# Gated linear attention and a three-way maxout FFN: units of 64 tokens of two batches in 64x64 array tiles, 32x32 blocks turned by VectorE, all engine orders fixed

## The chip, the cores and the metric

The kernel runs on one core of a Trainium2 chip. The metric is device time in microseconds (us), as the median of several executions. A core has five engines with an instruction stream each: TensorE (PE in the profile; PEld is its weight load), VectorE (DVE), ScalarE (ACT), GpSimd (POOL) and SyncE (SP), which here does little but issue DMA transfers. SyncE's issues stand in the traces shown here in the order of its program.

## The reference

Attention with a gated state, per batch and head, followed by an FFN whose hidden layer is the largest of three products. All inputs are float32 or float64 arrays as below; the weights arrive in float64 and are rounded on the chip.

```python
# B, H, S, D = 4, 8, 768, 48;  d_model = H*D = 384;  d_ff = 768
f = 1.0 / (1.0 + np.exp(-f_logit))
for t in range(S):
    state = f[:, :, t, :, None] * state + np.einsum('bhd,bhe->bhde', k[:, :, t], v[:, :, t])
    y[:, :, t] = np.einsum('bhd,bhde->bhe', q[:, :, t], state)
x = np.ascontiguousarray(y.transpose(0, 2, 1, 3)).reshape(B * S, H * D)      # 3072 x 384
h = np.maximum(np.maximum(x @ w1, x @ w2), x @ w3)
out = h @ w_out
```

## The kernel before

The sequence is cut into chunks of C = 128 tokens. One unit is one chunk of one batch; there are 24 units, and four units (the four batches at the same chunk) make one group of 512 tokens for the FFN. Per unit: f, k and q are loaded with tokens on partitions and turned by TensorE (`gates`), a scan gives the running products of the gates, a reciprocal gives the scaled keys `kh`; then come scores (`pairs`), values, the state and its read (`outputs`). The result is moved into `xT`, the FFN's input, by ten DMA transfers per unit. The FFN is a generator: each `next` (called by `fill`) emits one step, so that a group's FFN is mixed among the attention units of the next group.

```python
def load(u):
    c, b = divmod(u, B)
    for nm, src in (("f", f_logit), ("k", k), ("q", q), ("v", v)):
        nc.sync.dma_start(out=pads[nm][u % NLD][:, :, 0:D], in_=src[b, :, c*C:(c+1)*C, :].rearrange("h t d -> t h d"))
# ... in outputs(u, xT):
    for hp in range(HP):
        for par in range(2):
            nc.tensor.matmul(y[par*DP:(par+1)*DP, hp, :], lhsT=v_ld[:, 2*hp+par, :], rhs=at[:, par, hp, :], ...)
# ... key state, state read, then:
    nc.scalar.copy(yT, y)
    for h in range(H):               # ten transfers per unit, over borders of 128 rows
        # ...
        nc.sync.dma_start(out=xT[row % 128:row % 128 + n, row // 128, b*C:(b+1)*C], in_=yT[p0:p0+n, h // 2, :])
# ... the main loop, orders left to the scheduler:
for u in range(NU):
    # ...
    fill(2); pairs(u); fill(1); outputs(u, xT)
    if u + NLD < NU: load(u + NLD)
    # ... gates of later units, three weight pieces rounded in the first group
    fill(2)
    if u % GRP == GRP - 1:
        for _ in pending: pass
        pending = ffn(u // GRP, xT)
```

Of the kernel before, what the change touches and what calls it, by code (L numbers as in the profile page):

```python
# [34 lines left out]
C = 128  # L35
DP = 64
# [7 lines left out]
def kernel(  # L44
# [15 lines left out]
    NCH = S // C  # L60
    NU = B * NCH
# [4 lines left out]
    GRP = B  # L66
    TOK = GRP * C

    const = ctx.enter_context(tc.tile_pool(name="const", bufs=1))
    ident = const.tile([128, 128], FP32, name="ident")  # L70
    make_identity(nc, ident)
    w_in = [const.tile([128, NK, DFF], FP32, name=f"w_in{i}") for i in range(3)]
# [3 lines left out]
    def fast():  # L76
        ctx = ExitStack()
        with ctx:
# [7 lines left out]
            mask = keep.tile([C, C], FP32, name="mask")  # L86
            nc.gpsimd.memset(mask, 1.0)
            nc.gpsimd.affine_select(out=mask, in_=mask, compare_op=ALU.is_ge, fill=0.0, base=0,
                                    pattern=[[1, C]], channel_multiplier=-1)


            floor = keep.tile([128, HP, C + 1], FP32, name="floor")
            nc.vector.memset(floor, P_FLOOR)
            nc.vector.memset(floor[:, :, 0], 1.0)
            gate_tiles = [keep.tile([128, HP, C + 1], FP32, name=f"gate{i}") for i in range(2)]
# [4 lines left out]
            ends = keep.tile([128, NU, HP], FP32, name="ends")  # L100

            NLD = 4
            pads = {}
            for nm, pad in (("f", GATE_PAD), ("k", 0.0), ("q", 0.0), ("v", 0.0)):
                pads[nm] = []
                for i in range(NLD):
                    t = keep.tile([C, H, DP], FP32, name=f"{nm}_ld{i}")
                    nc.vector.memset(t[:, :, D:DP], pad)
                    pads[nm].append(t)


            def load(u):
                c, b = divmod(u, B)
                for nm, src in (("f", f_logit), ("k", k), ("q", q), ("v", v)):
                    nc.sync.dma_start(out=pads[nm][u % NLD][:, :, 0:D],
                                      in_=src[b, :, c * C:(c + 1) * C, :].rearrange("h t d -> t h d"))


            pieces = [(w_in[i][:, :, j * 128:(j + 1) * 128],
                       src[:, j * 128:(j + 1) * 128].rearrange("(kt p) c -> p kt c", p=128))  # L120
                      for j in range(NJ) for i, src in enumerate((moe_w1, moe_w2, moe_w3))]
            pieces += [(w_out[:, j:j + 1, :], moe_w_out[j * 128:(j + 1) * 128, :].rearrange("(j p) c -> p j c", p=128))
                       for j in range(NJ)]
            N = DM
            RAW = 6
            raw = {}

            def load_weight(n):
                if n >= len(pieces):
                    return  # L130
                dst, src = pieces[n]
                if src.dtype == FP32:
                    nc.sync.dma_start(out=dst, in_=src)
                else:
                    raw[n] = work.tile([128, 2 * N], U32, name="raw", bufs=RAW)
                    nc.sync.dma_start(out=raw[n].rearrange("p (a c) -> p a c", a=dst.shape[1]),
                                      in_=src.bitcast(U32))

            def round_weight(n):
                if n in raw:  # L140
                    dst = pieces[n][0]
                    words = raw.pop(n).rearrange("p (n two) -> p n two", two=2)
                    lo, hi = words[:, :, 0], words[:, :, 1]


                    top = work.tile([128, N], U32, name="top_bits")
                    nc.vector.tensor_scalar(top, hi, 3, 0x3FFFFFF8, op0=ALU.logical_shift_left, op1=ALU.bitwise_and)  # L147
                    nc.vector.scalar_tensor_tensor(top, hi, 0xC0000000, top, op0=ALU.bitwise_and, op1=ALU.bitwise_or)  # L148

                    rest = work.tile([128, N], U32, name="rest_bits")  # L150
                    nc.scalar.activation(rest, lo, AF.Copy, scale=2.0 ** -29)
                    nc.vector.tensor_tensor(top, top, rest, op=ALU.add)  # L152


                    size = work.tile([128, N], FP32, name="size")
                    nc.scalar.activation(size, hi.bitcast(FP32), AF.Square)
                    a = dst.shape[1]
                    nc.vector.scalar_tensor_tensor(dst, size.rearrange("p (a c) -> p a c", a=a), HI_MIN ** 2,
                                                   top.bitcast(FP32).rearrange("p (a c) -> p a c", a=a),
                                                   op0=ALU.is_ge, op1=ALU.mult)  # L160
                load_weight(n + RAW)


            def transposed(x):
                t = ps_tr.tile([128, HP, C], FP32, name="tr")
# [3 lines left out]
                return t  # L169

            ready = {}

            def gates(u):
                f_ld, k_ld, q_ld = (pads[nm][u % NLD] for nm in "fkq")
                tr_f = transposed(f_ld)
                gate = gate_tiles[u % 2]
                nc.scalar.activation(gate[:, :, 1:], tr_f, AF.Sigmoid)  # L177
                scan = work.tile([128, HP, C + 1], FP32, name="prod", bufs=3)
                nc.vector.tensor_tensor_scan(scan.rearrange("p a t -> p (a t)"), gate.rearrange("p a t -> p (a t)"),  # L179
                                             floor.rearrange("p a t -> p (a t)"), 1.0, op0=ALU.mult, op1=ALU.max)  # L180
                prod = scan[:, :, 1:]
                inv = work.tile([128, HP, C], FP32, name="inv")
                nc.vector.reciprocal(inv, prod)  # L183
                tr_k = transposed(k_ld)
                kt = work.tile([128, HP, C], FP32, name="kt")
                nc.scalar.copy(kt, tr_k)
                tr_q = transposed(q_ld)
                qt = work.tile([128, HP, C], FP32, name="qt")
                nc.scalar.copy(qt, tr_q)  # L189
                kh = work.tile([128, HP, C], FP32, name="kh", bufs=3)  # L190
                nc.gpsimd.tensor_tensor(kh, kt, inv, op=ALU.mult)  # L191
                qh = work.tile([128, HP, C], FP32, name="qh", bufs=3)
                nc.gpsimd.tensor_tensor(qh, qt, prod, op=ALU.mult)  # L193
                nc.gpsimd.tensor_copy(ends[:, u, :], prod[:, :, C - 1])  # L194
                ready[u] = (prod, kh, qh)

            def pairs(u):
                c = u // B
                prod, kh, qh = ready[u]
                a = ps_a.tile([C, 2, HP, C], FP32, name="a")  # L200
                for hp in range(HP):
                    for par in range(2):
                        r = slice(par * DP, par * DP + D)
                        nc.tensor.matmul(a[:, par, hp, :], lhsT=kh[r, hp, :], rhs=qh[r, hp, :],  # L204
                                         start=True, stop=True)
                at = work.tile([C, 2, HP, C], FP32, name="at")
                for par in range(2):
                    nc.vector.tensor_tensor(at[:, par], a[:, par],  # L208
                                            mask.unsqueeze(1).to_broadcast([C, HP, C]), op=ALU.mult)
                ks = None  # L210
                if c < NCH - 1:
                    tr_s = ps_tr.tile([C, HP, 128], FP32, name="tr")
                    for hp in range(HP):
                        nc.tensor.transpose(tr_s[:, hp, :], kh[:, hp, :], ident)  # L214
                    ks = work.tile([C, H, DP], FP32, name="ks")
                    nc.scalar.copy(ks.rearrange("s h d -> s (h d)"), tr_s.rearrange("s a d -> s (a d)"))  # L216
                ready[u] = (prod, qh, at, ks)

            states = [[keep.tile([128, HP, D], FP32, name=f"st{b}_{i}") for i in range(2)] for b in range(B)]

            def outputs(u, xT):
                c, b = divmod(u, B)
                prod, qh, at, ks = ready.pop(u)
                v_ld = pads["v"][u % NLD]
                st, st_new = states[b][c % 2], states[b][(c + 1) % 2]
                y = ps_y.tile([128, HP, C], FP32, name="y")
                for hp in range(HP):
                    for par in range(2):
                        nc.tensor.matmul(y[par * DP:(par + 1) * DP, hp, :], lhsT=v_ld[:, 2 * hp + par, :],  # L229
                                         rhs=at[:, par, hp, :], start=(hp == 0),  # L230
                                         stop=(c == 0 and hp == HP - 1), skip_group_check=True)
                if c < NCH - 1:
                    ds = ps_tr.tile([128, HP, D], FP32, name="tr")
                    for hp in range(HP):
                        for par in range(2):
                            nc.tensor.matmul(ds[par * DP:(par + 1) * DP, hp, :], lhsT=ks[:, 2 * hp + par, :],  # L236
# [322 lines left out]
```

## Time and profile before

| | before |
|---|---|
| median of 4 runs (of the rounds shared with the changed kernel) | 555.74 us (554.5 to 556.89) |
| span of the profiled run, mean granted TensorE clock | 553.3 us, 0.964 |
| first FFN matmul starts | 68.7 us |
| first group of units after that, then four groups | 82.6, then 83.4 each |
| last FFN and tail | 61.9 and 6.7 |

The prediction shows how these come out of the profile.

### The profile page before, as it was taken

Reading aid. Unit: us, or ns where it says so; the run is one execution under the profiler, and the core shown is the slowest. Engines: PE = TensorE matmul, PEld = TensorE weight load, DVE = VectorE, ACT = ScalarE, POOL = GpSimd, SP = SyncE. Lnnn points to the kernel's source line nnn. Section 1 sums busy time; section 2 is a strip of 40 time slices with the busy share of each in tenths; the row PEclk is TensorE's granted clock in tenths of the full one; section 3 lists DMA queues with packets and bytes.
Section 4 is the critical chain, followed back from the end, with each engine's and each line's share of the span. In section 5 each row is a group of like instructions: output and inputs, shape, how many; then the busy total and the mean of one; then the engine's idle time right before and its main releaser. Section 6 shows DMA issues: what was moved, by which queue, how often, KB each, and the median us from issue to landing. Waiting matters only on the chain.

```text
span 553.3 us, 7062 instructions
## 1 busy us (share of the span) xinstructions
PE 525.2 (95%) x2714; PEld 297.6 (54%) x2714; DVE 248.2 (45%) x322; ACT 121.9 (22%) x225; POOL 66.5 (12%) x82
## 2 busy tenths in 40 slices
PE   5886899998999999999999999999999999999995
PEld 4664644545655555555555555655655555544452
DVE  7799935995055435054346054346044242011210
ACT  3353422551122112122212122212122210110010
POOL 4322200220011001011011011011011010000000
PEclk9686889997999999999999999999999999999998
DMA  9857676353232213123122223130200000100001
GB/s 182 228 113 154 157 202 156 103 138 62 78 73 57 62 35 63 58 58 72 41 51 53 64 65 71 28 64 11 58 28 15 12 9 10 57 14 1 0 14 50
DMA packets 124458, 38.31 MB, mean 69 GB/s; under 512 B 104448, under 2 KB 123648, under 8 KB 124416
## 3 DMA queue, kind: packets, MB, share of 16 engines
q1 hardware_dynamic: 124416, 37.77, 28.4%
q8 instruction: 23, 0.38, 0.3%
q14 instruction: 19, 0.16, 0.1%
HBM read 28.31 MB, written 4.72 MB: 60 GB/s over the span
## 4 chain that ended last, share of the span: by engine, by line
PE 85%; DVE 8%; issue 3%; ACT 2%; POOL 1%; DVEq 0%; ACTq 0%; POOLq 0%
PE p L273 47%; PE p L286 17%; PE tr L168 5%; PE a L204 4%; PE y L229 4%; PE y L242 3%; DVE inv L183 3%; PE tr L236 2%; PE tr L214 2%; DVE prod L179 1%; POOL kh L191 1%; DVE at L208 1%; DVE top_bits L148 1%; DVE top_bits L152 1%; DVE top_bits L147 1%
## 5 line engine op out<-in xcount | busy, mean ns | idle before, releaser
L273 PE MATMUL p<-xT,w_in 128*128 128x512 f32 x648 | 292.7, 598 | 0.0
L273 PEld LDWEIGHTS p<-xT,w_in 128*128 128x128 f32 x648 | 118.0, 190 | 126.4 <-issue 123.7
L286 PE MATMUL p<-w_out,hm 128*128 128x384 f32 x288 | 96.3, 495 | 0.0
L183 DVE RECIPROCAL inv<-prod 128x512 f32<-128x512 f32 x24 | 80.4, 3351 | 1.8
L286 PEld LDWEIGHTS p<-w_out,hm 128*128 128x128 f32 x288 | 55.2, 193 | 39.1 <-issue 3.3
L279 DVE TENSOR_TENSOR top<-p,top 128x512 f32<-128x512 f32 x36 | 24.6, 682 | 112.4 <-PE p L273 112.4
L179 DVE TENSOR_TENSOR_SCAN prod<-gate,floor 128x516 f32<-128x516 f32 x24 | 29.5, 1229 | 90.0 <-ACT gate L177 88.0
L277 ACT COPY top<-p 128x512 f32<-128x512 f32 x36 | 21.1, 586 | 129.0 <-PE p L273 128.9
L279 DVE TENSOR_TENSOR hm<-p,top 128x512 f32<-128x512 f32 x36 | 24.6, 683 | 48.6 <-PE p L273 48.3
L194 POOL COPY ends<-prod 128x4 f32<-128x4 f32 x24 | 5.1, 213 | 321.4 <-DVE prod L179 321.4
L204 PEld LDWEIGHTS a<-qh,kh 48*128 48x128 f32 x384 | 25.3, 193 | 25.9 <-issue 16.8
L204 PE MATMUL a<-qh,kh 48*128 48x128 f32 x384 | 31.4, 295 | 8.0 <-POOL kh L191 8.0
L191 POOL TENSOR_TENSOR kh<-kt,inv 128x512 f32<-128x512 f32 x24 | 32.1, 1336 | 37.8 <-DVE inv L183 36.7
L208 DVE TENSOR_TENSOR at<-a,mask 128x512 f32<-128x512 f32 x48 | 31.0, 681 | 9.7 <-PE a L204 9.7
L229 PE MATMUL y<-at,v_ld 128*64 128x128 f32 x384 | 32.4, 301 | 2.5 <-DVE at L208 2.2
L229 PEld LDWEIGHTS y<-at,v_ld 128*64 128x64 f32 x384 | 24.3, 150 | 18.7 <-issue 14.1
L245 ACT COPY yT<-y 128x512 f32<-128x512 f32 x24 | 14.0, 585 | 83.7 <-PE y L242 78.7
L289 ACT COPY o<-p 128x384 f32<-128x384 f32 x24 | 11.5, 479 | 88.8 <-PE p L286 88.8
L193 POOL TENSOR_TENSOR qh<-qt,prod 128x512 f32<-128x512 f32 x24 | 28.3, 1181 | 21.2 <-ACT qt L189 21.2
L242 PE MATMUL y<-qh,st 48*48 48x128 f32 x320 | 23.0, 283 | 0.0
L216 ACT COPY ks<-tr 128x512 f32<-128x512 f32 x20 | 11.7, 586 | 50.1 <-PE tr L214 50.1
L177 ACT ACTIVATE gate<-tr 128x512 f32<-128x512 f32 x24 | 14.3, 597 | 36.5 <-PE tr L168 36.5
(45 smaller groups left out, 282.4 us busy)
## 6 DMA issues: line engine op xcount, KB each, us to landing
raw<-in_moe_w_dram SPq DMA_DIRECT2D x18, 384.0 KB, 4.8
f_ld<-in_f_logit_dram SPq DMA_DIRECT2D x24, 192.0 KB, 2.9
k_ld<-in_k_dram SPq DMA_DIRECT2D x24, 192.0 KB, 3.4
q_ld<-in_q_dram SPq DMA_DIRECT2D x24, 192.0 KB, 3.5
v_ld<-in_v_dram SPq DMA_DIRECT2D x24, 192.0 KB, 3.0
out_dram<-o SPq DMA_DIRECT2D x24, 192.0 KB, 1.9
xT<-yT SPq DMA_DIRECT2D x144, 24.0 KB, 1.8
raw<-in_moe_w_out_dram SPq DMA_DIRECT2D x6, 384.0 KB, 3.6
```

The lines of the kernel that those rows point to most:

```text
L168: nc.tensor.transpose(t[:, hp, :], flat[:, hp * 128:(hp + 1) * 128], ident)
L179: nc.vector.tensor_tensor_scan(scan.rearrange("p a t -> p (a t)"), gate.rearrange("p a t -> p (a t)"), floor.rearrange("p a t -> p (a t)") ...
L183: nc.vector.reciprocal(inv, prod)
L191: nc.gpsimd.tensor_tensor(kh, kt, inv, op=ALU.mult)
L193: nc.gpsimd.tensor_tensor(qh, qt, prod, op=ALU.mult)
L204: nc.tensor.matmul(a[:, par, hp, :], lhsT=kh[r, hp, :], rhs=qh[r, hp, :], start=True, stop=True)
L208: nc.vector.tensor_tensor(at[:, par], a[:, par], mask.unsqueeze(1).to_broadcast([C, HP, C]), op=ALU.mult)
L229: nc.tensor.matmul(y[par * DP:(par + 1) * DP, hp, :], lhsT=v_ld[:, 2 * hp + par, :], rhs=at[:, par, hp, :], start=(hp == 0), stop=(c == 0 ...
L242: nc.tensor.matmul(y[r, hp, :], lhsT=st[r, hp, :], rhs=qh[r, hp, :], start=False, stop=(hp == HP - 1), skip_group_check=True)
L273: nc.tensor.matmul(p, lhsT=w_in[i][:, kt, j * 128:(j + 1) * 128], rhs=xT[:, kt, :], start=(kt == 0), stop=(kt == NK - 1))
L279: nc.vector.tensor_tensor(hm[:, j, :] if i == 2 else top, p, top, op=ALU.max)
L286: nc.tensor.matmul(p[:, 0:DM], lhsT=hm[:, j, i * C:(i + 1) * C], rhs=w_out[:, j, :], start=(j == 0), stop=(j == NJ - 1))
```

## The change

The intent is to make TensorE's attention work cheaper and the start shorter. A unit becomes 64 tokens of two batches, so that each small product has four 64x64 array tiles to run in. From unit 8 on, f, k and q are loaded as blocks of 32x32 so that VectorE can turn them instead of TensorE. Rows of `xT` and the input weights are permuted, so that most of the result reaches `xT` by ScalarE copies and only six small transfers per unit are left. The weights' add moves to GpSimd. And everything stands in one manual schedule: the program's order is each engine's order.

```diff
-C = 128
+C = 64                                 # UT = 2*C token rows of a unit; GRP = 4
 # ...
+            elif u % 2 == 0:           # BY_ROWS = 8: later units by 32x32 blocks, two units at once
+                for n in range(C // 32):
+                    for par in range(2):
+                        for e0, w in ((0, 32), (32, D - 32)):
+                            nc.sync.dma_start(out=blocks[nm][u // 2 % 2][p0:p0 + 32, n, :, 0:w], in_=...)
 # ... in round_weight:
-    nc.vector.tensor_tensor(top, top, rest, op=ALU.add)
+    nc.gpsimd.tensor_tensor(top, top, rest, op=ALU.add)
 # ... in products(u):
-    tr_k = transposed(k_ld); nc.scalar.copy(kt, tr_k)
+    turned(t, block(nm, u))            # nc.vector.transpose, units 8 and later
 # ... every attention product:
-    for hp in range(HP):
-        for par in range(2):
+    FOUR = [(par, a) for a in range(2) for par in range(2)]
+    for hp in range(HP):
+        for par, a in FOUR:
 # ... in finish(u, xT):
-    ten nc.sync.dma_start(out=xT[...], in_=yT[...])
+    for par in range(2):               # after ScalarE copies of the other rows
+        for i in range(NK):
+            nc.sync.dma_start(out=xT[p0 + D:p0 + DP, i, t0:t0 + UT], in_=last[...])
 # ... the order:
+with tc.manual_schedule():
+    # loads of units 0 to 3, four weight pieces; gates(0); gates(1)
+    for u in range(GRP):
+        keys(u)
+        if u > 1: finish(u - 1, xT)
+        pairs(u)
+        if u + 2 < GRP: gates(u + 2)
+        values(u)
+        load(u + GRP); load_v(u + GRP)
+        # finish(0) at u == 0; three weight pieces at u == 1
+    finish(GRP - 1, xT)
+    pending = ffn(0, xT)
+    # ...
+    for u in range(GRP, NU):
+        if BY_ROWS <= u + 2 < NU and u % 2 == 0: load(u + 2)
+        # load_v(u + 2)
+        fill(2 if u % 2 and u < NU - GRP else 1)
+        keys(u)
+        if u > GRP: finish(u - 1, xT)
+        if u % GRP == 0:
+            if u > GRP:
+                fill(99)
+                pending = ffn(u // GRP - 1, xT)
+            xT = new_xT()
+        pairs(u)
+        # ... sigmoids, products, values, quotients of units u and u + 1, with fill(1) between
```

(The lines of the diff are shortened; the cuts are marked by `# ...`.)

## The prediction

> **What bounds the kernel now.** I read the page from the top: busy shares first, then the slices, then the group rows.
>
> ```profile
> PE 525.2 (95%) x2714; PEld 297.6 (54%) x2714; DVE 248.2 (45%) x322; ACT 121.9 (22%) x225; POOL 66.5 (12%) x82
> ...
> PE   5886899998999999999999999999999999999995
> ...
> DVE  7799935995055435054346054346044242011210
> ...
> PEclk9686889997999999999999999999999999999998
> ```
>
> TensorE is the bound, except in the first eight or so slices, where the PE digits and the granted clock drop and VectorE reads 9. Next, who fills TensorE:
>
> ```profile
> L273 PE MATMUL p<-xT,w_in 128*128 128x512 f32 x648 | 292.7, 598 | 0.0
> ...
> L286 PE MATMUL p<-w_out,hm 128*128 128x384 f32 x288 | 96.3, 495 | 0.0
> L183 DVE RECIPROCAL inv<-prod 128x512 f32<-128x512 f32 x24 | 80.4, 3351 | 1.8
> ```
>
> Means of pipelined matmuls overlap, so I use starts. The stretch table has TensorE busy for all 333.45 us of 151.3 to 484.75, and records of the FFN start 0.429 us (512 columns) and 0.323 us (384 columns) apart. One 512-token group is 108 x 0.429 + 48 x 0.3267 (15.68 us by the chain) = 62.0 us, six of them 372. None of it changes. The ledger of the 553.3 us span:
> - 68.7 us before the first FFN matmul;
> - 82.6 us to the end of the first group (151.3), while VectorE also rounds weights;
> - four groups of 83.4 us (333.45 / 4), each FFN mixed with four attention units;
> - the last FFN alone, 61.9 us, and a tail of 6.7.
>
> So attention costs TensorE (83.4 - 62.0) / 4 = 5.35 us per unit. The timeline of one steady unit shows of what:
>
> ```profile
> 157.68 1.16 PE L204 MATMUL a<-qh,kh 48*128 48x128 f32 x16
> 158.77 0.66 PE L214 MATMUL tr<-ident,kh 128*128 128x128 f32 x4
> 159.26 2.74 PE L273 MATMUL p<-xT,w_in 128*128 128x512 f32 x6
> 161.94 1.09 PE L229 MATMUL y<-at,v_ld 128*64 128x128 f32 x16
> 162.86 0.62 PE L236 MATMUL tr<-v_ld,ks 128*64 128x48 f32 x16
> 163.41 1.08 PE L242 MATMUL y<-qh,st 48*48 48x128 f32 x16
> 164.42 5.42 PE L273 MATMUL p<-xT,w_in 128*128 128x512 f32 x12
> 169.67 0.60 PE L168 MATMUL tr<-ident,f_ld 128*128 128x128 f32 x4
> ```
>
> From start to next start: pair scores 1.09 us, key transposes 0.49, values 0.92, state update 0.55, state read 1.01, and three input transposes of 0.44. Single records show two array tiles at work: two starts 7 ns apart, then 103 to 105 ns to the next two (128 columns), or 52 ns with 48 columns, where the weight load of 64 columns repeats every 58 ns. A change of tile size costs about 0.2 us at each side (203 and 206 ns around the pair scores).
>
> **What the Trainium skill says.** "TensorE: Matmul & The Clock Gate", Part 3, has tiles of the array running together, some 4 ns apart; the trace agrees with 7 ns for two tiles and has no case of four. The same page, section LDWEIGHTS, puts a load at columns / 1.2, 53 ns for 64 columns; the 58 ns agree. "TensorEngine Tiling (Array Packing)", Key Properties, says that a mode switch drains the array; the 0.2 us agree. "Vector Engine (DVE) Microarchitecture Reference", section 3.8, has the 32x32 transpose sustain one element per cycle per lane; no run shows it yet.
>
> **The change, part by part.**
>
> *64x64 tiles.* A unit has 128 token rows as before (64 of two batches), so 24 units and six FFN groups stay. Each attention product becomes 16 matmuls, 32 records instead of 16, of 64 (or 48) columns in four tiles. If four run together at the 58 ns of a 64-column load, a product takes 32 / 4 x 58 = 0.46 us; four products 1.86. Key transposes stay, 0.44. Finish and scores share one mode, so four switches remain, 0.8. Total 3.1 us. For later units the input transposes (1.31) are gone; early ones have 4.4. Against 5.35: 2.25 us less per later unit, so a steady group needs 62.0 + 12.4 = 74.4 us, **9 us less in each of four groups**.
>
> *Turned inputs.* VectorE gets three transposes of 512 elements. As estimate I take the 0.68 us of its 512-element row, so 2.0 us per unit. Per unit then: 2.0 + scan 1.23 + two half reciprocals 3.5 + mask 1.25 + state 1.1 + FFN maxima 2.05 = 11.1 us, against 18.6 of TensorE. It stays hidden.
>
> *Start.* Before, VectorE did seven scans and reciprocals and nine weight pieces ahead of the first FFN; three gates (4.6 us each) and six pieces (2.2 us each) of that weren't needed yet. Now it is four gates and three pieces. Walking VectorE's fixed order from the same first scan at 5.6 us (gates 4.75, mask 1.25, state 0.55 to 1.1, pieces 2.75), I get the last values at 43 us and, after copies and the transfers into xT, the first FFN matmul at **50 us instead of 68.7**.
>
> *First FFN group.* It now carries 12 pieces, nine of double size. The add goes to GpSimd, but with fixed order VectorE waits for it. GpSimd's 512-element row is 1.18 to 1.34 us, so an add of 768 is about 1.9 (estimate), and a double piece holds VectorE for 0.83 + 2.1 + 0.99 + 0.97 = 4.9 us, 3 x 2.75 + 9 x 4.9 = 52 in all. With gates 26, masks and states 9, maxima 8 it is 95 us against TensorE's 80: this group becomes VectorE's, **97 us instead of 82.6**. The gain of the start is mostly given back here.
>
> *Group boundaries.* xT now comes by ACT copies and six transfers per unit instead of ten. But no FFN step is left when the last unit of a group finishes. The issue queue needs about 0.7 us for each xT transfer (ten in 7.06 us), then 1.8 to land: 6 x 0.7 + 1.8 + 0.65 of copies is 6.7 us, 0.5 of it under the scores. Worse, at even units 24 block loads and two v loads stand in the same queue ahead of these transfers, at 0.44 us each another 11 us. Read strictly, TensorE idles about 14 us at three boundaries and about as long at unit 8. The DMA engines have room (26% busy in steady groups).
>
> *Sum.* 50 + 97 + 10 (unit 8) + 4 x 74.4 + 3 x 4 + 61.9 + 6.7 = 535; timed runs lie 3.5 above the span: **539 us**. The 10 and the 4 are my choice, below the strict reading: the step counts (two in odd units, fewer near the end) look laid out to cover such waits.
>
> **Rivals.**
> 1. *The transfers into xT become the wait.* For it: one in-order queue, no spare FFN steps, 0.44 to 0.7 us per issue in the trace. Against: the queue may run ahead. With 14 us four times (4 + 3 x 10 more) the time is about 573, slower.
> 2. *Four tiles don't run together.* Then a product takes about 0.93 us, a unit 4.9, and the gain of a steady group falls to 2 us: about 567. For it: the trace shows only two tiles at once. Against: the two-tile cases already overlap fully, both by row and by column.
> 3. *Everything is covered:* no idling at boundaries and a first group at TensorE's 80 us: about 500. Against: the 2.1 us waits of VectorE on GpSimd sit in a fixed order.
> 4. *VectorE bounds steady groups* if a turned 512 elements takes far over 0.68 us. At 2 us each a unit needs 15, still under 18.6: no effect.
>
> **Range and chances.** From 539, rivals 1 and 2 in part give 572, a part of rival 3 gives 508. Faster by over 2% is below 546. The steady saving is the surest term, the boundaries the weakest, and half of a strict reading of them already eats it: faster 0.58, same 0.27, slower 0.15.
>
> **What would show each step.** Tiles: in a steady unit four starts some 7 ns apart, then about 40 ns; a product of 32 records in 0.46 us. Later units: no L168 transposes; a VectorE TRANSPOSE group of 48 instructions near 0.65 us. Start: first FFN matmul near 50 us. First group: VectorE waits of about 2 us on GpSimd's add, end near 147. Boundaries: TensorE idle ahead of the first FFN matmul of a group, released by the xT transfer, with a dip of PE and PEclk in the slices. The prediction is wrong if a boundary idles over 10 us, if products stay near 0.9 us, or if VectorE paces steady groups.

## More of the kernel before

```profile
PE 85%; DVE 8%; issue 3%; ACT 2%; POOL 1%; DVEq 0%; ACTq 0%; POOLq 0%
...
xT<-yT SPq DMA_DIRECT2D x144, 24.0 KB, 1.8
```

TensorE is nearly the whole chain, and SyncE's queue (SPq) isn't in it at all. The transfers into `xT` are there, 240 in all (the page lists the 144 of 24 KB; 96 smaller ones are left out), but nothing that ends last waits for them.

## The result, and the profile after

The changed kernel takes **628.30 us** (median of 4 runs, 627.45 to 630.64), against 555.74 us before on the same chip. The ratio is 1.1313, with a 95% interval of 1.1268 to 1.1358: slower by 13%. The output is correct.

From the page of the changed kernel: TensorE's busy time (and the other engines'); the PE row and the granted clock in 40 slices (15.7 us each); the chain that ended last; and the group of input matmuls of the FFN, whose last column is TensorE's idle time just before them and what ended most of it.

```profile
PE 484.0 (77%) x4067; PEld 259.5 (41%) x4067; DVE 261.3 (42%) x321; ACT 127.6 (20%) x297; POOL 100.8 (16%) x139
...
PE   5830168597991799990999990999981999999995
...
PEclk9765597887996799996899995899995999999998
...
PE 66%; SPq 12%; DVE 9%; issue 4%; POOL 3%; DMA 2%; ACT 2%; DVEq 0%; POOLq 0%; ACTq 0%
...
L373 PE MATMUL p<-xT,w_in 128*128 128x512 f32 x648 | 304.4, 624 | 95.5 <-DMA xT<-last 87.9
```

TensorE is busy 41 us *less* than before (484.0 against 525.2), but its row has five holes: a 0 and a 1 in the start, then a 1 at unit 8 and a 0, a 0 and a 1 at the later boundaries. SPq, absent from the chain before, is now 12% of it. There are 531 issues in all instead of 384, although `xT` takes 144 instead of 240. And one row holds most of TensorE's idle time (142.9 us of the span): before the FFN's input matmuls it idles 95.5 us, 87.9 of it for the transfers of `last` into `xT`. Before, that column read 0.0.

The holes one by one, from TensorE's order in time: the idle time in square brackets ahead of the first FFN matmul is 26.92 us in the start, 11.71 at unit 8 and 15.97, 17.16 and 16.18 at the other three boundaries, 87.9 in sum. One boundary in detail; first TensorE, then SyncE's issues (start, length, line, what, how many):

```profile
282.69 0.65 PE L301 MATMUL a<-qh,kh 48*64 48x64 f32 x32
299.31 7.70 PE L373 MATMUL p<-xT,w_in 128*128 128x512 f32 x12 [15.97 <-DMA xT<-last]
```

```profile
279.71 4.37 SPq L158 DMA_DIRECT2D f_ld<-in_f_logit_dram  x8
284.18 4.15 SPq L158 DMA_DIRECT2D k_ld<-in_k_dram  x8
288.42 4.15 SPq L158 DMA_DIRECT2D q_ld<-in_q_dram  x8
292.67 1.46 SPq L145 DMA_DIRECT2D v_ld<-in_v_dram  x2
294.22 1.22 SPq L395 DMA_DIRECT2D out_dram<-o  x2
295.54 3.73 SPq L362 DMA_DIRECT2D xT<-last  x6
```

The scores of unit 12 end at 283.3 us, and the next FFN needs `xT`. The six transfers that it waits for are issued only from 295.54 to 299.27, because 24 block loads for units that come later, two loads of v and two outputs stand ahead of them in the same queue, at 0.5 to 0.7 us each. The DMA engines are not full: their mean busy share is 0.30 over these groups, though 0.73 from 283.4 to 295.5 us, while the block loads run. Experiments 1 and 2 move the same bytes and separate the queue from the engines.

The start has the same form. Three of SyncE's rows, and TensorE:

```profile
51.99 3.87 SPq L362 DMA_DIRECT2D xT<-last  x6
...
62.26 3.74 SPq L362 DMA_DIRECT2D xT<-last  x6
...
71.58 3.74 SPq L362 DMA_DIRECT2D xT<-last  x6
```

```profile
75.40 4.44 PE L373 MATMUL p<-xT,w_in 128*128 128x512 f32 x6 [26.92 <-DMA xT<-last]
```

SyncE issues from 0.82 to 75.32 us nearly without a gap. There are 112 issues: 60 row loads of units 0 to 7 (ScalarE issues the other four, k and q of unit 0), 28 transfers of weights, because the permuted rows split each input piece into four, and 24 transfers into `xT`. Between two of the rows shown lie eight row loads of units that nobody needs yet, 5.4 us each time.

What worked as hoped is the cheaper unit. In a steady stretch:

```profile
226.39 0.60 PE L288 MATMUL tr<-ident,kh 128*128 128x128 f32 x4
226.92 0.66 PE L348 MATMUL y<-qh,st 48*48 48x64 f32 x32
227.40 0.65 PE L301 MATMUL a<-qh,kh 48*64 48x64 f32 x32
227.98 5.42 PE L373 MATMUL p<-xT,w_in 128*128 128x512 f32 x12
```

A product of 32 records goes from start to next start in 0.48 to 0.58 us. Single records show starts 7, 7 and 6 ns apart and then 38 ns: four tiles at work, four records per 58 ns.

### The profile page after: what moved, and what is told of

Read it like the earlier page. It is cut to its first block, busy times and chain, and to the rows that moved or that the text cites. A ratio compares the mean times of both kernels' runs of the same rounds, so it can differ in the third digit from the quotient of the medians.

```text
span 626.9 us, 10135 instructions
## 1 busy us (share of the span) xinstructions
PE 484.0 (77%) x4067; PEld 259.5 (41%) x4067; DVE 261.3 (42%) x321; ACT 127.6 (20%) x297; POOL 100.8 (16%) x139
## 4 chain that ended last, share of the span: by engine, by line
PE 66%; SPq 12%; DVE 9%; issue 4%; POOL 3%; DMA 2%; ACT 2%; DVEq 0%; POOLq 0%; ACTq 0%
PE p L373 43%; PE p L388 13%; SPq L158 5%; DVE inv L274 4%; SPq L145 3%; POOL top_bits L212 2%; PE y L348 2%; SPq L362 2%; PE y L318 2%; PE tr L288 2%; PE a L301 2%; DMA xT<-last 1%; PE y L327 1%; DVE top_bits L213 1%; DVE prod L255 1%
## 5 line engine op out<-in xcount | busy, mean ns | idle before, releaser
L373 PE MATMUL p<-xT,w_in 128*128 128x512 f32 x648 | 304.4, 624 | 95.5 <-DMA xT<-last 87.9
L388 PE MATMUL p<-w_out,hm 128*128 128x384 f32 x288 | 95.5, 488 | 1.5 <-DVE hm L379 1.5
L274 DVE RECIPROCAL inv<-prod 128x256 f32<-128x256 f32 x48 | 82.5, 1734 | 0.3
L275 POOL TENSOR_TENSOR kh<-kt,inv 128x256 f32<-128x256 f32 x48 | 36.2, 754 | 157.2 <-DVE inv L274 157.2
L304 DVE TENSOR_TENSOR at<-a,mask 128x512 f32<-128x512 f32 x24 | 16.5, 687 | 51.8 <-PE a L301 51.8
L213 DVE SCALAR_TENSOR_TENSOR top_bits<-raw,top_bits 128x768 uint32<-128x768 uint32 (+1 forms) x15 | 12.0, 800 | 61.2 <-POOL top_bits L212 61.2
L255 DVE TENSOR_TENSOR_SCAN prod<-gate,floor 128x520 f32<-128x520 f32 x24 | 29.7, 1238 | 7.8 <-issue 4.5
L212 POOL TENSOR_TENSOR top_bits<-top_bits,rest_bits 128x768 uint32<-128x768 uint32 (+1 forms) x15 | 22.2, 1483 | 62.7 <-ACT rest_bits L211 43.0
L288 PE MATMUL tr<-ident,kh 128*128 128x128 f32 x88 | 16.3, 317 | 17.7 <-POOL kh L275 17.7
L318 PE MATMUL y<-at,v_ld 64*64 64x64 f32 x768 | 18.0, 236 | 9.8 <-issue 8.8
L290 ACT COPY ks<-tr 128x512 f32<-128x512 f32 x22 | 12.9, 585 | 60.2 <-PE tr L288 60.2
L318 PEld LDWEIGHTS y<-at,v_ld 64*64 64x64 f32 x768 | 14.6, 144 | 25.0 <-issue 23.6
L357 ACT COPY xT<-y 64x192 f32<-64x192 f32 (+1 forms) x72 | 22.7, 316 | 1.3
L354 ACT COPY last<-y 64x64 f32<-64x64 f32 (+1 forms) x72 | 15.0, 209 | 23.8 <-DMA xT<-last 12.4
```

Source lines behind the costliest of these rows:

```text
L212: nc.gpsimd.tensor_tensor(top, top, rest, op=ALU.add)
L255: nc.vector.tensor_tensor_scan(scan.rearrange("p x t -> p (x t)"), gate.rearrange("p x t -> p (x t)"), floor.rearrange("p x t -> p (x t)") ...
L274: nc.vector.reciprocal(d["inv"][:, a], d["prod"][:, a])
L275: nc.gpsimd.tensor_tensor(d["kh"][:, :, a, :], d["kt"][:, a], d["inv"][:, a], op=ALU.mult)
L288: nc.tensor.transpose(tr_s[:, hp, :], kh[:, hp].rearrange("p a t -> p (a t)"), ident)
L318: nc.tensor.matmul(y[o:o + DP, a, hp * C:(hp + 1) * C], lhsT=v_ld[s, 2 * hp + par, :], rhs=d["at"][s, par, hp, :], start=(hp == 0), stop=F ...
```

## The experiments

Fourteen kernels were run, each against the kernel before on the same chip. All gave correct results. Edits are against the changed kernel. Three ideas stood against each other at first: that the queue of issues holds up the transfers into `xT`; that the fixed order of the engines costs the time as such; and that the small tiles or VectorE's new work cost it.

### 1. The transfers into xT from another queue

```diff
-                        nc.sync.dma_start(out=xT[p0 + D:p0 + DP, i, t0:t0 + UT],
+                        nc.scalar.dma_start(out=xT[p0 + D:p0 + DP, i, t0:t0 + UT],
```

> The six transfers per unit into xT are issued from ScalarE's queue instead of the one that all loads share. Theory Q (the shared issue queue is the bound, about 0.65 us per issue): the first FFN matmul moves from 75.4 us to about 56, the idle ahead of each group's first FFN matmul falls from 11.7 / 16.0 / 17.2 / 16.2 us to 5 to 7, and the time falls from 628 to about 575. Rival L (the transfer itself, issue to landing, is what takes the time): idle stays near 16 us and the time stays within 1% of 628. Rival V (VectorE's fixed order paces the start): the first FFN matmul stays at 70 us or later.

Measured: 586.81 us (585.95 to 588.36), ratio to before 1.0573 (1.0522 to 1.0623). The first FFN matmul comes at 58.7 us instead of 75.4, with 6.7 us of idling instead of 26.9, and the boundaries idle some 5 us instead of 12 to 17. Moving 144 issues, and nothing else, gives back 41 of the 73 us. The queue is a cause. The expected 575 was missed by 12 us; experiment 14 shows what this edit costs elsewhere.

### 2. The same by order alone

```diff
-                    if BY_ROWS <= u + 2 < NU and u % 2 == 0:
-                        load(u + 2)
 # ...
                         finish(u - 1, xT)
+                    if BY_ROWS <= u + 2 < NU and u % 2 == 0:
+                        load(u + 2)
```

> The 24 block loads of an even unit are issued behind the transfers into xT instead of ahead of them; nothing else moves. Theory Q: each of the four boundaries loses about 13 us of queue, so the idle falls to 3 to 6 us, with about 2 us each from the clock that no longer drops; the start stays at 75 us; the time is about 585. Rival L: idle and time unchanged. Rival B (the DMA engines, not the queue, are full with the small blocks): the idle shrinks but the block loads then arrive late and VectorE's turning waits, with less than half of the gain.

Measured: 589.95 us (587.38 to 590.55), ratio 1.0604 (1.0552 to 1.0657). The row of the FFN's input matmuls now reads:

```profile
L373 PE MATMUL p<-xT,w_in 128*128 128x512 f32 x648 | 307.5, 629 | 54.3 <-DMA xT<-last 46.7
```

The block loads now stand behind the transfers into `xT`. Of the 46.7 us the boundaries have 4.4, 4.7, 5.7 and 4.7, and the start, which this edit doesn't touch, still has 27.18. So the block loads' place ahead of the transfers at four boundaries costs 38 us of the timed 628, and the order within one queue settles it without a second queue. What is left there is about what six issues of 0.62 us and 1.8 us to land make, 5.5.

### 3. The fixed order removed

```diff
-            with tc.manual_schedule():
+            if True:
```

> Only the fixing of the engine orders is taken away; the framework orders the instructions as in the kernel before. Theory O (the fixed order is to blame): the time falls to 560 or less, with the boundaries filled by other work. Theory Q: the same number of issues goes through the same queue, so the first FFN matmul stays above 65 us, but the boundaries may be filled; 585 to 620.

Measured: 618.86 us (616.6 to 620.26), ratio 1.1134 (1.1076 to 1.1191). TensorE's input matmuls have no idle time put down to transfers into `xT`, and FFN groups start 82 us apart instead of 92: the scheduler's own order has no such holes at the boundaries. But it puts the first FFN matmul at 107 us. The fixed order as such isn't what costs the time; each of the two orders loses it in a different place.

### 4. The add back on VectorE

```diff
-                    nc.gpsimd.tensor_tensor(top, top, rest, op=ALU.add)
+                    nc.vector.tensor_tensor(top, top, rest, op=ALU.add)    # after the masked or, as before
```

> The add of the weight rounding goes back from GpSimd to VectorE. Theory: in the first FFN group a double piece holds VectorE for 3.4 us instead of 4.6 (it waits 2.0 to 2.4 us for GpSimd now, an add on VectorE should take about 1.0), so the group of 110.3 us shrinks by about 10 to 14 us, the start (75.4 us, bound by the queue) doesn't move, and the time is about 616. Rival: the group is paced by TensorE's low clock (0.86) or by weight arrival, and the time stays within 3 us.

Measured: 623.26 us (621.57 to 624.46), ratio 1.1227 (1.1175 to 1.1278): 5.0 us under the changed kernel, less than expected. The first group, from first FFN matmul to last, takes 102 us instead of 110.3. The waits that it takes away are these, in the changed kernel (who waited for whom: us in total, times, longest):

```profile
DVE top_bits L213 <- POOL top_bits L212: 61.2, 15, 33.6
```

More than half of the 61.2 us is a single wait of 33.6. By size, 39.5 us belong to the six small pieces and 21.8 to the nine double ones, 2.4 us each; the single long wait reaches across the hole in the start and costs nothing of its own. The start and the boundaries idle as before (27.5 us in the start), so it is a term of the first group only.

### 5. The four tiles one after another

```diff
-                for hp in range(HP):
-                    for par, a in FOUR:
+                for par, a in FOUR:
+                    for hp in range(HP):        # in all four products
```

> The same 64x64 matmuls, but all of one array tile one after another instead of the four tiles in turn. Theory T (tiles overlap only because neighbouring instructions go to different tiles): a product of 32 records takes up to 32 x 58 ns = 1.86 us instead of 0.48, a unit grows by up to 5.5 us and the time by up to 100 us. Rival: the array's own queue looks ahead far enough to keep four tiles busy in any order, and a product stays near 0.5 us.

Measured: one run of 677.45 us, state unknown, so the time isn't used. TensorE's group of the score matmuls, in the changed kernel and here (busy us, mean ns of one):

```profile
L301 PE MATMUL a<-qh,kh 48*64 48x64 f32 x768 | 18.1, 241 | 0.0
```

```profile
L301 PE MATMUL a<-qh,kh 48*64 48x64 f32 x768 | 43.1, 248 | 0.0
```

The mean of one record hardly differs, the busy time is 2.4 times as long: a product takes about 1.3 us from start to next start instead of 0.48. Four tiles run together only where the program names them in turn; the order of the inner loops is worth 4 x 0.8 = 3.2 us per unit. The changed kernel has it right, so the tiles aren't what slows it.

### 6. No 32x32 blocks

```diff
-            BY_ROWS = 8
+            BY_ROWS = 24                # and load(u + 2) for every unit from 8 on; no block padding
```

> All 24 units loaded by rows and transposed on TensorE; no 32x32 blocks. TensorE pays 12 transposes, about 1.3 us, in 16 more units: +21 us. Theory Q: only 8 issues of 0.65 us instead of 26 of 0.55 stand ahead of the transfers into xT at a boundary, so the idle of 16 to 17 us falls to about 7, three times, and at unit 8 from 12 to about 5: -35 us with the clock. Net about 614. Rival (blocks are a plain gain of 21 us and the queue doesn't matter): about 649.

Measured: 613.39 us (611.99 to 616.64), ratio 1.1062 (1.1009 to 1.1115), as expected. TensorE turns all inputs again, with 12 row loads per two units instead of 24 block loads. The boundaries idle 3.2, 7.1, 7.0 and 6.4 us. The FFN groups come 88 us apart (199.15, 287.30, 375.64, 463.53) instead of 92. So on this order the turned blocks lose: what they save TensorE is less than what their issues cost. Behind the transfers (experiment 2, 589.95 us) the same blocks beat this kernel; row loads in that place were not tried.

### 7. Spare FFN steps at the boundaries

```diff
-                    fill(2 if u % 2 and u < NU - GRP else 1)
+                    fill(2 if u % 2 and u < GRP else 1)
```

> One FFN step instead of two ahead of odd units in all groups, so that two output steps (3.9 us each) are left to run behind the last unit of each group while the transfers into xT are under way. Theory Q: the idle at three boundaries falls from 16 to 17 us to about 9, the one at unit 8 hardly moves (the first group has no spare step), and the time falls by about 21 to 25 us to 605. Rival: the step only moves the idle to another place (keys wait for GpSimd's product): time within 1% of 628.

In this loop u is never below GRP, so the edit means one step ahead of every unit. Measured: 606.59 us (605.1 to 610.48), ratio 1.0939 (1.0881 to 1.0996), as expected. With fewer steps spent early, the last steps of an FFN run while the transfers for the next one are awaited: idling of 7.8, 9.3 and 8.9 us at the last three boundaries instead of 16 to 17. Unit 8's boundary gains nothing, because the first group still has no step to spare: TensorE gets there earlier and idles 18.0 us instead of 11.7, and the next FFN starts at 207.1 us as before (207.4).

### 8. Four edits together

Edits 1, 2, 4 and 7 in one kernel.

> Transfers into xT on ScalarE's queue, block loads behind them, the add back on VectorE, and spare steps: all four. If the parts add up: first FFN matmul at 58 us, no idle over 2 us at the last three boundaries, steady groups of 75 us as predicted from TensorE's work, a first group of about 115 us to the next group's first matmul. 58 + 115 + 3 x 75 + 74 + 69 + 3 = 544. If the first group stays near 130: 559.

Measured: 548.72 us (548.36 to 549.01), ratio 0.9877 (0.9843 to 0.9911), so 1.2% under the kernel before. The last three boundaries don't idle. What is left is the first group: 114 us with its boundary, against 76 of a steady one.

### 9. Fewer issues in the start: a miss

```diff
-                    load(u + GRP)
+                    load(u + GRP, nc.scalar)     # k and q of units 4 to 7: 16 of the 112 issues
```

> The changed kernel with one edit: the k and q loads of units 4 to 7, in the start, are issued by ScalarE. That takes 16 of the 112 issues that stand ahead of, or are, the last transfers into xT off the SyncE queue, and nothing else. Theory Q (the start ends when the SyncE queue has issued its list, 0.65 us each): the first FFN matmul moves from 75.4 by 16 x 0.65 = 10.4 to about 65 us, and the time from 628 to about 618. Rival D (the start is limited by the transfers themselves, or by VectorE's chain): same bytes, same VectorE order, so the first FFN matmul stays at 75 and the time at 628. ScalarE may be held up by its own issues, 16 x 0.65 us = 10 us spread over four units; if that showed, less than 10 us would be gained.

Measured: 628.42 us (627.34 to 629.91), ratio 1.1315 (1.1274 to 1.1356). Nothing moved: first FFN matmul at 75.96 us. Taken alone this speaks for the rival, that the transfers themselves or VectorE set the start. But SyncE's waits of the first 80 us show where the freed time went; the changed kernel has none of the four rows below:

```profile
SPq L196 <- DMA k_ld<-in_k_dram: 4.1, 4, 3.0
SPq L145 <- DMA k_ld<-in_k_dram: 3.5, 2, 3.3
SPq L362 <- DMA k_ld<-in_k_dram: 2.6, 2, 1.9
SPq L196 <- DMA v_ld<-in_v_dram: 1.6, 2, 0.9
```

Issues of SyncE (weights, rows, `xT`) now wait for landings, above all of the k loads that ScalarE issued. All waits of SyncE for landings sum to 16.3 us in this stretch (the four rows are 11.8 of them), against 1.0 in the changed kernel. They outweigh the 16 issues of 0.68 us, 10.9. In the single records every issue names one of eight completion semaphores, and both engines take theirs from the same eight. That an issue waits until the last transfer with its semaphore has landed fits all of this; it is read from the records and not tested by itself.

### 10 and 11. Two attempts on the first group: misses

Edit 10 adds to kernel 8 a fifth raw buffer and rounds weight pieces 3 to 5 ahead of the first FFN step. Edit 11 adds to kernel 10 the k and q loads of units 4 to 7 issued by GpSimd.

```diff
-            RAW = 4
+            RAW = 5
 # ...
                 finish(GRP - 1, xT)
+                for n in range(3, 6):
+                    round_weight(n)
 # ...
-                        if g == 0 and (step < 6 or step % 2 == 0):
-                            round_weight(3 + step if step < 6 else 6 + step // 2)
+                        if g == 0 and step % 2 == 0:
+                            round_weight(6 + step // 2)
 # edit 11 also:
-                    load(u + GRP)
+                    load(u + GRP, nc.gpsimd)
```

> The four edits of the earlier combined run (548.7 us) and one more for what was left of its loss, the first FFN group: a fifth raw buffer, and weight pieces 3 to 5 rounded between the last finish and the first FFN step instead of one per step at the first six steps; the later nine pieces then come at every second step. If the gaps of TensorE in the first group (113.7 us with its boundary against 76.1 of a steady group) come from VectorE and ScalarE handling pieces at every step, the first group shrinks by 5 to 10 us: 538 to 544 us. If they come from the weight pieces' late arrival, nothing is gained: 547 to 550 us. The kernel before is expected at 556.

> As the run before it, and the k and q loads of units 4 to 7 are issued by GpSimd, which has time in the start. Theory Q: 16 fewer issues ahead of the weights and outputs in the SyncE queue, so weight pieces 5 and later are issued up to 10 us earlier and the waits on them in the first group shrink: 530 to 540 us. If GpSimd's own products wait behind its issues, the start grows instead and the gain is gone: 545 to 555 us.

Measured: 551.91 us (550.7 to 554.06), ratio 0.9936 (0.9907 to 0.9966), and 548.50 us (544.34 to 550.3), ratio 0.9862 (0.9823 to 0.9901). Neither beats kernel 8. In kernel 10 TensorE idles 10.06 us, from 63 to 73 us, for ScalarE's sigmoid of unit 4: the three pieces now stand ahead of it in ScalarE's order. ScalarE itself waits there, 6.6 and 3.2 us, for transfers of weights to land, which is the other outcome that was named before the run. The wait was only moved. GpSimd's queue made it 3.4 us less, by the medians; what held up the rest of the expected gain in kernel 11 was not followed.

### 12. Fewer issues in the start, in one queue

Edit 9 had changed two things at once: the list ahead of the last transfers, and the number of queues. This one changes the list alone.

```diff
                     values(u)
-                    load(u + GRP)
-                    load_v(u + GRP)
 # ...
                 finish(GRP - 1, xT)
+                for u in range(GRP, 2 * GRP):
+                    load(u)
+                    load_v(u)
                 pending = ffn(0, xT)
```

> The changed kernel with one edit: in the start, the 32 loads of units 4 to 7 are issued behind the last transfers into xT instead of between the transfers; all stay in the SyncE queue. Theory Q (the list of issues ahead of the last xT transfer sets the start): 32 x 0.68 = 21.8 us less, so the first FFN matmul at 54 to 57 us instead of 75.4 and the time near 610, if the first group doesn't give it back; the waits of SyncE issues for landings of another queue, 14 us in the run with ScalarE, don't appear. Rival D (the transfers themselves, or VectorE's chain, set the start): first FFN matmul at 70 us or later, time 624 to 630.

Measured: 609.94 us (609.76 to 611.08), ratio 1.0982 (1.0951 to 1.1013). SyncE and TensorE in the start:

```profile
40.84 14.17 SPq L362 DMA_DIRECT2D xT<-last  x18
55.10 1.35 SPq L145 DMA_DIRECT2D f_ld<-in_f_logit_dram  x2
```

```profile
55.09 5.04 PE L373 MATMUL p<-xT,w_in 128*128 128x512 f32 x6 [5.20 <-DMA xT<-last]
```

Thirty-two issues fewer ahead, and the first FFN matmul comes 20.3 us earlier (0.63 per issue), inside the expected 54 to 57. The same bytes are moved and VectorE's order is the same, so the rival of experiment 9 falls for these 20 us. It is the list of issues that set the start. The time fell by 18.4 us.

### 13 and 14. The combined kernel with one queue and with two

Kernel 13 has edits 2, 4, 7 and 12; kernel 14 has edit 1 as well.

> Loads of the start behind the last xT transfers, later block loads behind finish's xT transfers, the add back on VectorE, spare FFN steps for the boundaries; everything in the one SyncE queue. Theory W (the combined version with ScalarE's queue, 548.7, loses time to waits between the two queues): here no SyncE issue waits for a landing of another queue, weight pieces come earlier, first FFN matmul at about 56, first group with boundary about 105, the rest as there: 535 to 545 us. Rival: one queue makes the boundaries idle 5 to 9 us each again, 550 to 570 us.

> As the run before it, but the transfers into xT are issued by ScalarE again. Theory W: the waits between the queues come back (over 10 us of SyncE waiting for xT landings in the first 120 us) and this is slower than the one-queue version in the first group, while the boundaries are as free as in the earlier combined run: 540 to 550 us. Rival (two queues are worth more than their waits): under the one-queue version by 5 us or more.

Measured: with one queue **536.49 us** (535.74 to 537.82), ratio 0.9655 (0.963 to 0.9681), faster than the kernel before by 3.5%. With two queues 551.12 us (548.84 to 552.29), ratio 0.9906 (0.9881 to 0.9931). So here a second queue costs 14.6 us. Two things in kernel 14's trace can be the reason. The first is SyncE's waits; here are those of the first 180 us (kernel 13's only waits for landings there are 8.0 us for weights):

```profile
SPq L196 <- DMA xT<-last: 27.8, 9, 11.2
SPq L145 <- DMA xT<-last: 17.5, 3, 10.5
SPq L158 <- DMA xT<-last: 11.2, 5, 8.6
```

Weights, row loads and block loads wait for landings of transfers that ScalarE issued: 56.5 us in sum. The second is ScalarE's own time. Issuing the six transfers of a unit keeps it some 4 us, and the next sigmoid or copy stands behind them in its order; over the whole run:

```profile
ACT sig L247 <- DMA xT<-last: 40.5, 11, 4.2
```

Kernel 13 has no such row; in the kernel of experiment 1 it is 57.2 us, 16 times. Of the 16.2 us between the two profiled spans, 6.0 are there by the scores of unit 4 (81.2 us against 75.3) and 6.4 by those of unit 8 (169.7 against 163.3). The other 10 come after that, where TensorE waits 6.1 us for VectorE, whose work on a unit starts from the late sigmoid, and for no transfer. So SyncE's waits aren't shown to be the whole reason; how much each of the two costs was not tested apart. In kernel 13 the row that lost 95.5 us reads:

```profile
L373 PE MATMUL p<-xT,w_in 128*128 128x512 f32 x648 | 297.0, 611 | 13.4 <-DMA xT<-last 9.9
```

And its steady stretches, each from scores to scores (span; PE busy and count; at the end the granted clock, DMA share and GB/s):

```profile
245.40:319.50 74.10, 74.10 (x696) 39.05 (x686) 41.11 (x48) 16.42 (x44) 11.74 (x16) 1.00 0.37 56
319.50:393.60 74.10, 74.10 (x692) 39.05 (x684) 41.13 (x48) 16.43 (x44) 11.74 (x16) 1.00 0.38 58
```

TensorE is busy throughout at full clock, and a group takes 74.1 us. The prediction's 74.4 was the length of a group that waits for nothing; the changed kernel had it in its tiles and hid it behind its queue and its step counts. Edits 2 and 12 were not run by themselves as a pair; from their single gains, 38.4 and 18.4 us, the order of the queue is worth about 57 of the 73 us (an estimate).

## Why the prediction was wrong

The prediction was 539 us and faster; the kernel takes 628.3 and is slower. Its ledger beside what the trace shows (us of the span):

| stretch | predicted | measured | difference |
|---|---|---|---|
| to the first FFN matmul | 50 | 75.4 | +25.4 |
| first group | 97 | 110.3 | +13.3 |
| boundary at unit 8 | 10 | 21.7 | +11.7 |
| three groups, each with its boundary | 3 x 78.4 = 235.2 | 91.9 + 93.2 + 91.7 = 276.8 | +41.6 |
| fourth group | 74.4 | 73.1 | -1.3 |
| last FFN and tail | 68.6 | 69.5 | +0.9 |
| sum | 535 | 626.8 | +91.6 |

**Right: the unit.** The tile product was predicted at 0.46 us and is 0.48 to 0.51 in steady units; a unit is near the 3.1 us. The fourth group took 73.1 us, and experiment 13 shows undisturbed groups of 74.1 against 74.4. The fear of rival 2, that four tiles don't run together, was unfounded with this loop order; experiment 5 shows that it holds with another.

**Right: the turned inputs.** The 48 block transposes take 669 to 706 ns on average, by input (0.68 predicted), and VectorE doesn't pace a steady group. The mask was counted too dear: 0.69 us per unit, not 1.25.

**Wrong: the boundaries.** This step had the mechanism and its size: "Read strictly, TensorE idles about 14 us at three boundaries and about as long at unit 8." The trace shows 16.0, 17.2 and 16.2, and 11.7 at unit 8. The step that failed is "The 10 and the 4 are my choice, below the strict reading: the step counts (two in odd units, fewer near the end) look laid out to cover such waits." At these four boundaries the step counts cover nothing: the FFN's steps are used up before the boundary, and experiment 7 shows that different counts would have covered 7 to 8 us at three of them. Only ahead of the last FFN are two steps held back, and there TensorE doesn't idle (no block loads are left there either). Two further terms were too low or missing. A block load was taken at 0.44 us and is 0.54 in the queue (12.9 us for 24); in the trace before, loads of the steady groups already took 0.37 to 0.78 us (seven issues from 236.8 to 258.9 us, 0.55 on average). And the clock falls during the wait: in the hole at unit 12 the granted clock is 0.50 from 286.9 us, 3.6 us after the last matmul, to 304.0. The twelve FFN matmuls after the hole took 7.70 us (7.2 to 7.6 after the other three), and twelve after no hole take 5.42, so each hole costs some 2 us more. The Trainium skill has this rule in "TensorE: Matmul & The Clock Gate", Part 1 (after an idle window of some 3.4 us the array is back at half rate); the trace agrees, and the prediction expected the dip but put no time on it. The prediction's own terms, 6.7 - 0.5 + 11, make 17 rather than its 14; the measured holes lie near 17. Rival 1 of the prediction, the transfers into `xT` behind other issues, is what happened. Its time, about 573, was too low because it kept the other terms.

**Wrong: the start.** "Walking VectorE's fixed order [...] I get the last values at 43 us and, after copies and the transfers into xT, the first FFN matmul at 50 us instead of 68.7". The walk itself was good: the values' matmuls of the fourth unit start at 45.8 us. What failed is the last clause, which gave the transfers some 7 us and forgot that their queue carries 112 issues by then. At 0.65 us each, where the prediction took 0.44 for a load, the queue alone is at 73 us (the trace: 75.3). The prediction had priced the queue for the boundaries and didn't do the same sum for the start. Experiment 12 shows it: 32 issues moved, 20.3 us gained.

**Wrong in size: the first group.** VectorE's waits on GpSimd's add were predicted at 2.1 us and are 2.0 to 2.4 for eight of the nine double pieces (4.7 for one); GpSimd's add of 768 took 1.81 us (1.9 predicted). With the add back on VectorE (experiment 4) the stretch is still 102 us, 5 over a prediction that had counted the add's waits in, so the waits aren't what was mis-sized, and the cause of the 13.3 us stays open. What the trace shows: TensorE is busy 89.2 of the 110.3 us (80 predicted) at a mean granted clock of 0.86, and VectorE only for 59.3. In experiment 13, with the add on VectorE and a first group that starts 22 us earlier, the stretch is still 106.9 us with TensorE busy for 87.8 of it.

**The range.** Rivals were weighed as if only one could be true. Here two terms fell the same way from one cause, the number of issues in one queue: start, unit 8 and boundaries are 78.7 of the 91.6 us. Not all of that is the queue's: at unit 8 TensorE also idles 5.9 us for `kh`, and experiment 2 brought the next FFN only 6.9 us forward there. The range ended at 572.

## What to carry to other kernels

Count the DMA issues of each queue as you count an engine's instructions: number times time per issue, in order, against the moment when each result is needed. A change that makes transfers smaller and more numerous has to be costed there first, and urgent transfers go ahead of loads that have time. A second issuing engine isn't a free way out: look at what the issues then wait for, and at what work of that engine then waits behind its issues, because here the same edits were 14.6 us faster in one well-ordered queue. And where your own strict sum gives a cost, keep it in the number unless you can point at what covers it.

## What the Trainium skill lacked or had wrong

- "DMA: Bandwidth & Descriptors", section "Issuing engines are not separate DMA queues", says that issuing from several engines saves only the time to initiate a transfer, "which is usually small relative to the DMA itself". Here issuing was the bound: 0.54 us per block load and 0.62 us per `xT` transfer, with a median of 1.8 us from issue of such a transfer to landing and a DMA share of 0.30 over these groups. Moving 144 issues to a second engine took the time from 628.3 to 586.8 us.
- I found no page that says that issues of one engine can wait for landings of transfers issued by another. The runs show it: in experiment 9 SyncE's issues waited 16.3 us for landings, in experiment 14 they waited 56.5 us for landings of ScalarE's transfers, and the one-queue kernel 13 has none of the latter.
- "TensorE: Matmul & The Clock Gate", Part 3, gives the overlap of array tiles, and says that matmuls start in program order, but gives no figure for a program that names one tile several times in a row. With the four tiles named in turn a product of 32 records took 0.48 us (starts 6 to 7 ns apart, not the 4 given there); with the same tile named several times in a row, about 1.3 (experiment 5, one run). In that run's records matmuls do start out of program order: at all 42 changes from the state read to the scores and from the values to the state update, one of the next product starts before the last of the one before it (at 237.38 us a score, ahead of state reads up to 237.55); in the changed kernel at none of 42.
